# Window attention feeding a mixture of attentions: the weighted values of stage 1 tied to those of stage 2, and the PSUM banks in two rings

## Chip, cores and metric

One Trainium2 chip, one core. Each kernel is one program on that core, inputs and outputs in HBM. The metric is the device time of one execution in microseconds, taken as the median of several executions; a profile is one more execution, recorded by the hardware profiler. The engines are named as in the profile: PE (TensorE, matmuls), PEld (TensorE's weight loads, which overlap PE), DVE (VectorE), ACT (ScalarE), POOL (GpSimd) and SP (SyncE, which issues the transfers). A matmul writes a bank of PSUM; there are eight banks of 128 partitions by 512 fp32 numbers, and only ACT and DVE read them here.

## What is computed

The reference, cut to its core (8 batches, 8 heads, 576 positions, heads of 64, 4 experts of which 2 count for each position):

```
# stage 1: causal attention in a window of 64, on q, k, v
scores = q @ k^T / 8 ; mask: 0 <= row - col < 64
x = softmax(scores) @ v                 # back to batch x 576 x 512
# stage 2: four full causal attentions on x, weighted by a gate
logits = x @ w_gate ; w = softmax over the best 2 of 4
for e in range(4):
    q, k, v = x @ wq[e], x @ wk[e], x @ wv[e]       # 512 -> 64
    a = softmax(q @ k^T / 8, causal over all 576)
    out += w[e] * (a @ v @ wo[e])                   # 64 -> 512
```

## The kernel before

**Stage 1** is cut into 72 groups `g` of four tiles (a tile is 64 query positions of a pair of heads), nine groups to a batch. `s1_qk` multiplies q by k into a PSUM tile `s1` (one bank), adds the mask and finds the row extreme on DVE (L200), takes the exponential on ACT (L210) and scales on POOL (L239). `s1_t` turns two groups' weights with PE transposes into a PSUM tile `t1`, which DVE copies out (L272). `s1_av` multiplies the turned weights by v: a group is eight matmuls (L300), two groups fill one PSUM tile `o1`, and ACT and DVE copy it out as a high and a low part, `xh` (L308) and `xl` (L309).

**Stage 2** takes a batch `b` in two pairs `pr` of experts. `s2_v`, `s2_k` and `s2_q` project `xh` and `xl` (PSUM tiles `v2ps`, `kps`, `qps`; L375 to L377, three matmuls for each product of split operands). `s2_s` makes the scores in eight PSUM tiles `s2` (L502, L503), which DVE masks (L516) and ACT exponentiates. `s2_t` turns the weights with PE transposes (L554, L576) in three tiles `t2` for part 0 of the rows and four for part 1, which ACT copies into `pt` (L561, L567, L578, L583). `s2_av` multiplies these by the values into a tile `o2` (L610), six matmuls for part 0 and ten for part 1, copied out by ACT and DVE as `yh` and `yl` (L616, L617). `s2_o` projects to the output (`ops`).

Both weighted-value steps write 64 rows at a time: their matmuls stand in the profile as `128*64`, all others as `128*128`. Each matmul of L194, L300, L497 and L610 runs as two passes and so has two rows.

**The order.** The last lines of the kernel give each step a time in units of half a batch: stage 2 by the table `POS`, stage 1 by its group number, `LEAD` and `LAG`; the steps are written in that order. A scheduler then orders each engine's instructions and picks the PSUM bank of each tile, out of the ring of its tag. A bank goes to the next tile when the last reader of the tile before is done. `PSB` sets the rings: three banks for `s1` and `s2`, two for `t1` and `t2`, two for the projections (`v2ps`, `kps`, `qps`, `ops`), and one for `o1` and `o2`. The step `s1_av` is moved beside the nearest `s2_av` if that is closer than `NEAR`.

Of the kernel before, what the change touches and what calls it, by code (L numbers as in the profile page):

```python
# [24 lines left out]
POS = {'T00': (-0.009, 0.006), 'T01': (-0.103, 0.133), 'T10': (-0.014, 0.353), 'T11': (0.115, 0.331), 'T1l': (0.403, 0.705), 'A00': (0.082, 0.139), 'A01': (0.077, 0.138), 'A10': (0.417, 0.468), 'A11': (0.358, 0.785), 'A1l': (0.672, 0.695), 'O0': (0.211, 0.52), 'O1': (0.518, 0.918), 'S00': (0.17, 0.403), 'S01': (0.032, 0.316), 'S10': (0.427, 0.819), 'S11': (0.736, 0.891), 'KQ1': (0.0, 1.0), 'V': (0.03, 0.476), 'G': (0.715, 0.852), 'GR': (0.713, 0.723), 'KQ0': (0.439, 0.939), 'VT': (0.084, 0.104)}
PSB = [3, 2, 2, 1]
SNAP = None
MODE = 'fold'
SPREAD = 'APVAVPPP'
LEAD = 12.0  # L30
WPOS = [-0.816, -0.201, -0.2, 1.723]
CPOS = -0.39
NEAR = 0.1
FIRST = 18
# [5 lines left out]
def window_attention_moe_attention(ctx: ExitStack, tc: tile.TileContext, qT, kT, vW,  # L40
# [93 lines left out]

    newer = const.tile([128, 64], mybir.dt.uint32, name="newer")
    nc.vector.tensor_scalar(newer, m_f[:, 0, 64:128], 0.5 * NEG, None, op0=OP.is_gt)

    tri = const.tile([128, 2, 128], F32, name="tri")
# [52 lines left out]
    def s1_qk(g):  # L191
        ps = psum.tile([128, 4, 128], F32, tag="s", bufs=PSB[0], name=f"s1_{g}")
        for i, p, b in tiles(g):
            nc.tensor.matmul(ps[:, i], lhsT=qbd_buf[p % 2][:, b], rhs=pairs[p][1][:, 64 * b:64 * b + 128],  # L194
                             start=True, stop=True)
        st = work.tile([128, 3, 4], F32, tag="st1", bufs=4, name=f"st1_{g}")
        if g < FIRST or MODE == "fold":
            sm = work.tile([128, 4, 2, 64], F32, tag="sm1", bufs=4, name=f"sm1_{g}")
            for i, p, b in tiles(g):
                nc.vector.tensor_tensor_reduce(out=sm[:, i].rearrange("r a c -> r (a c)"), in0=ps[:, i],  # L200
                                               in1=win[:, int(b == 0)], scale=-0.125, scalar=3.0e38,
                                               op0=OP.add, op1=OP.min, accum_out=st[:, 0, i:i + 1])
            if g < FIRST:
                pt = sm.rearrange("r t a c -> r t (a c)")
            else:
                pt = work.tile([128, 4, 64], F32, tag="p1", bufs=4, name=f"p1_{g}")

                nc.vector.tensor_tensor(pt, sm[:, :, 0], sm[:, :, 1], op=OP.min)  # L208
            for i in range(4):
                nc.scalar.activation(pt[:, i], pt[:, i], AF.Exp, bias=st[:, 0, i:i + 1], scale=-1.0,  # L210
                                     accum_out=st[:, 1, i:i + 1])
        else:
            pt = work.tile([128, 4, 64], F32, tag="p1", bufs=4, name=f"p1_{g}")

            firsts = [i for i, p, b in tiles(g) if b == 0]
            cuts = [-1] + firsts + [4]
            for i in firsts:
                nc.gpsimd.memset(pt[:, i], NEG)
            for lo, hi in zip(cuts, cuts[1:]):
                if hi > lo + 1:  # L220
                    nc.scalar.activation(pt[:, lo + 1:hi], ps[:, lo + 1:hi, 0:64], AF.Copy)
            nc.vector.copy_predicated(pt, newer[:, None, :].to_broadcast([128, 4, 64]), ps[:, :, 64:128])
            nc.vector.tensor_reduce(st[:, 0], pt, axis=AX.X, op=OP.max)
            if MODE == "batch":
                nc.gpsimd.tensor_tensor(pt, pt, st[:, 0, :, None].to_broadcast([128, 4, 64]), op=OP.subtract)
                nc.scalar.activation(pt, pt, AF.Exp, scale=0.125)
                nc.vector.tensor_reduce(st[:, 1], pt, axis=AX.X, op=OP.add)
            else:
                nc.vector.tensor_scalar(st[:, 0], st[:, 0], -0.125, None, op0=OP.mult)
                for i in range(4):  # L230
                    nc.scalar.activation(pt[:, i], pt[:, i], AF.Exp, bias=st[:, 0, i:i + 1], scale=0.125,
                                         accum_out=st[:, 1, i:i + 1])
        nc.vector.tensor_scalar_add(st[:, 2], st[:, 1], 1e-9)
        nc.vector.reciprocal(st[:, 2], st[:, 2])  # L234
        if g >= FIRST and MODE == "batch":
            nc.gpsimd.tensor_tensor(pt, pt, st[:, 2, :, None].to_broadcast([128, 4, 64]), op=OP.mult)
        else:
            for i in range(4):
                (nc.vector if g < FIRST and i < 1 else nc.gpsimd).tensor_scalar(pt[:, i], pt[:, i], st[:, 2, i:i + 1],  # L239
                                                                                1.0, op0=OP.mult, op1=OP.mult)  # L240
        P1[g] = pt
        for i, p, b in tiles(g):
            if b == BLK - 1 and p < 2:
                spread_q(p + 2)
            elif b == BLK - 1 and p + 2 < NB * NP:
                load_pair(p + 2)

    def s1_t(g):

        k = g % 9  # L250
        if k % 2 == 0 and k != 8:
            return
        gs = [g - 1, g] if k % 2 else [g]
        t = work.tile([128, 4, 2, 128], F32, tag="pt1", bufs=2, name=f"pt1_{g}")
        if g < FIRST:
            for x, y in enumerate(gs):
                pt = P1.pop(y)
                ps = psum.tile([128, 4, 128], F32, tag="t", bufs=PSB[1], name=f"t1_{y}")
                for i in range(4):
                    nc.tensor.transpose(ps[:, i], pt[:, i], ident)  # L260
                nc.scalar.activation(t[:, 2 * x:2 * x + 2].rearrange("r a e c -> r (a e) c"), ps, AF.Copy)
        else:
            n = 2 * len(gs)
            ps = psum.tile([128, 4, 128], F32, tag="t", bufs=PSB[1], name=f"t1_{g}")
# [223 lines left out]
    def s2_s(b, pr, k):  # L488
# [181 lines left out]
    for g in range(NG1):  # L670
# [76 lines left out]
```

## Time and profile before

| | |
|---|---|
| median of 3 runs | 525.08 us (524.7 to 525.42) |
| the profiled execution | 524.21 us, of which the span from first to last instruction is 522.5 us |
| busy in the span | PE 503.6 us, PEld 447.9, DVE 435.2, ACT 379.7, POOL 229.4 |
| DMA | 51.25 MB, 98 GB/s on average |

How to read it: the busy time of an engine is the time in which it had an instruction in hand. A PE row's end is modelled, and rows overlap in the pipeline, so starts, and steps from one start to the next, say more than durations. Waits are told of the engine that sat idle and of the instruction whose end released it. Where PE waits for an operand or a bank, the wait is longest seen on PEld, whose rows come first.

### The profile page before, as it was taken

To read this page: it belongs to the slowest core of one execution; us is meant where nothing else is said; L and a number is where in the kernel's file an instruction comes from. 1 tells how busy PE (TensorE), PEld (TensorE's weight loads), DVE (VectorE), ACT (ScalarE), POOL (GpSimd) and SP (SyncE) were. 2 spreads that over 40 slices of the span, in tenths; PEclk is the share of its full clock that TensorE was granted. 3 is DMA by queue.
4 is the path that set the end of the run, shared out by engine and by line. 5 is a ranking of instruction groups with operands and counts; after the bars stand their busy time and mean duration, and the time that the engine had idled before them with its cause. 6 is when DMAs were issued, how large, how long until landed. Compare 5 with 4: busy or idle time off the path is not lost.

```text
span 522.5 us, 14102 instructions
## 1 busy us (share of the span) xinstructions
PE 503.6 (96%) x4588; PEld 447.9 (86%) x4588; DVE 435.2 (83%) x1921; ACT 379.7 (73%) x1431; POOL 229.4 (44%) x611
## 2 busy tenths in 40 slices
PE   5999999999999999999999999999999999999996
PEld 5889998888889889988888888988888988998874
DVE  7787888989979898998988988999898998666652
ACT  6998897776676957678495875867767694758572
POOL 8666364444453343622454433444445243233330
PEclk9999999999999999999999999999999999999999
DMA  8963441322613324133341426213261101100103
GB/s 313 299 204 92 146 141 50 92 59 80 180 50 94 115 93 134 44 101 108 112 111 42 127 78 171 88 48 95 87 180 50 46 11 53 41 2 21 62 2 100
DMA packets 49754, 51.25 MB, mean 98 GB/s; under 512 B 35472, under 2 KB 35984, under 8 KB 49680
## 3 DMA queue, kind: packets, MB, share of 16 engines
q1 hardware_dynamic: 49680, 50.35, 32.1%
q8 instruction: 36, 0.59, 0.5%
q14 instruction: 38, 0.31, 0.2%
HBM read 40.90 MB, written 9.44 MB: 96 GB/s over the span
## 4 chain that ended last, share of the span: by engine, by line
PE 61%; ACT 19%; DVE 14%; issue 3%; POOL 1%; DMA 0%; POOLq 0%; DVEq 0%; ACTq 0%
PE o L610 8%; PE s L194 7%; PE t L554 7%; ACT p L210 6%; PE o L300 4%; PE s L502 4%; ACT p L525 3%; PE s L503 3%; PE ops L375 2%; PE kps L376 2%; PE ops L377 2%; PE kps L377 2%; DVE p L516 2%; PE kps L375 2%; PE ops L376 2%
## 5 line engine op out<-in xcount | busy, mean ns | idle before, releaser
L239 POOL TENSOR_SCALAR p<-p,st 128x64 f32<-128x64 f32 x216 | 64.0, 318 | 92.3 <-DVE st L234 54.6
L545 POOL TENSOR_SCALAR p<-p,r 128x192 f32<-128x192 f32 (+3 forms) x128 | 74.6, 597 | 50.0 <-DVE r L541 13.6
L210 ACT ACTIVATE p<-p,st 128x64 f32<-128x64 f32 x216 | 72.3, 337 | 27.1 <-DVE p L208 21.9
L194 PE MATMUL s<-k,qbd 128*128 128x128 f32 x540 | 75.5, 283 | 5.6 <-POOL qbd L94 5.6
L272 DVE TENSOR_TENSOR pt<-t,tri 64x512 f32<-64x512 f32 (+1 forms) x120 | 76.0, 633 | 5.6 <-PE t L268 3.1
L516 DVE CUSTOM_DVE_ANT_0 p<-s,causal 128x320 f32<-128x320 f32 (+3 forms) x160 | 73.4, 471 | 6.3 <-PE s L503 5.0
L200 DVE CUSTOM_DVE_ANT_0 sm<-s,win 128x128 f32<-128x128 f32 x288 | 69.7, 283 | 7.9 <-PE s L194 4.9
L194 PEld LDWEIGHTS s<-k,qbd 128*128 128x128 f32 x540 | 69.8, 197 | 6.6 <-POOL qbd L94 5.6
L554 PE MATMUL t<-ident,p 128*128 128x128 f32 x384 | 59.7, 279 | 3.3 <-ACT pt L567 1.5
L520 ACT ACTIVATE p<-p,r 128x192 f32<-128x192 f32 (+2 forms) x96 | 53.4, 558 | 10.6 <-DVE r L516 10.1
L472 POOL TENSOR_SCALAR qs<-qz 64x256 fp32r<-64x256 f32 x64 | 25.6, 400 | 72.5 <-ACT qz L470 69.0
L610 PE MATMUL o<-pt,v 128*64 128x256 f32 (+3 forms) x512 | 53.5, 340 | 0.9 <-DVE xl L309 0.8
L502 PE MATMUL s<-ks,qz 128*128 128x256 f32 (+2 forms) x160 | 53.4, 345 | 0.4 <-DVE r L516 0.3
L610 PEld LDWEIGHTS o<-pt,v 128*64 128x64 f32 x512 | 36.6, 136 | 19.7 <-ACT pt L578 2.0
L554 PEld LDWEIGHTS t<-ident,p 128*128 128x128 f32 x384 | 42.9, 140 | 11.8 <-ACT pt L583 3.3
L470 ACT ACTIVATE qz<-qps 64x256 fp32r<-64x256 f32 x64 | 24.2, 378 | 34.3 <-DVE qs L471 18.3
L503 PE MATMUL s<-ks,qs 128*128 128x256 f32 (+2 forms) x160 | 48.1, 312 | 0.0
L300 PEld LDWEIGHTS o<-pt,v 128*64 128x64 f32 x1152 | 37.0, 137 | 7.4 <-issue 1.4
L300 PE MATMUL o<-pt,v 128*64 128x64 f32 x1152 | 42.6, 225 | 0.4 <-DVE xl L309 0.3
L210 ACT ACTIVATION_READ_ACCUMULATOR p<-p,st 128x1 f32 x216 | 40.6, 188 | 0.0
L375 PE MATMUL kps<-xh,wkhi 128*128 128x320 f32 (+1 forms) x128 | 39.1, 306 | 0.1
L375 PE MATMUL qps<-xh,wqhi 128*128 128x320 f32 (+1 forms) x128 | 38.6, 302 | 0.2 <-DVE ks L462 0.2
(148 smaller groups left out, 1431.3 us busy)
## 6 DMA issues: line engine op xcount, KB each, us to landing
v<-in_vW_dram SPq DMA_DIRECT2D x32, 576.0 KB, 4.4
k<-in_kT_dram SPq DMA_DIRECT2D x30, 320.0 KB, 3.8
out_dram<-out SPq DMA_DIRECT2D x32, 256.0 KB, 2.2
qbd<-in_qT_dram SPq DMA_DIRECT2D x56, 144.0 KB, 3.5
out_dram<-out SPq DMA_DIRECT2D x8, 128.0 KB, 2.4
p<-in_kT_dram SPq DMA_DIRECT2D x2, 320.0 KB, 7.5
q<-in_qT_dram SPq DMA_DIRECT2D x2, 288.0 KB, 3.5
p<-in_qT_dram SPq DMA_DIRECT2D x2, 288.0 KB, 7.2
```

The lines of the kernel that those rows point to most:

```text
L194: nc.tensor.matmul(ps[:, i], lhsT=qbd_buf[p % 2][:, b], rhs=pairs[p][1][:, 64 * b:64 * b + 128], start=True, stop=True)
L200: nc.vector.tensor_tensor_reduce(out=sm[:, i].rearrange("r a c -> r (a c)"), in0=ps[:, i], in1=win[:, int(b == 0)], scale=-0.125, scalar=3 ...
L210: nc.scalar.activation(pt[:, i], pt[:, i], AF.Exp, bias=st[:, 0, i:i + 1], scale=-1.0, accum_out=st[:, 1, i:i + 1])
L239: (nc.vector if g < FIRST and i < 1 else nc.gpsimd).tensor_scalar(pt[:, i], pt[:, i], st[:, 2, i:i + 1], 1.0, op0=OP.mult, op1=OP.mult)
L272: nc.vector.tensor_mul(t[64 * w:64 * w + 64, :n, e], ps[r, :n], tri[r, w, None, :].to_broadcast([64, n, 128]))
L300: nc.tensor.matmul(o[64 * h:64 * h + 64, 4 * (k % 2) + i], lhsT=pairs[p][2][:, h, b], rhs=t[:, i, 64 * h:64 * h + 64], start=True, stop=True)
L375: nc.tensor.matmul(ps, lhsT=ah, rhs=bh, start=first, stop=False)
L502: nc.tensor.matmul(out, lhsT=QZ[pr][:, e, q], rhs=rhs, start=True, stop=False)
L516: nc.vector.tensor_tensor_reduce(out=dst, in0=ps[:, col:col + n], in1=mask, scale=1.0, scalar=3.0e38, op0=OP.add, op1=OP.min, accum_out=least)
L545: nc.gpsimd.tensor_scalar(p, p, r2[:, 3, x:x + 1], 1.0, op0=OP.mult, op1=OP.mult)
L554: nc.tensor.transpose(ps[:, col:col + 128], P2[part][:, at:at + 128], ident)
L610: nc.tensor.matmul(o[64 * h:64 * h + 64, q0:n], lhsT=V2[b % 2][:, c, 2 * pr + h], rhs=PT2[part][:, h, x:x + w], start=c == 0, stop=c == le ...
```

## The change

Three things, in the planner and in the tags; what is computed is the same.

1. From batch 2 on, four of the five `s1_av` steps of a batch are no longer placed by their own time but directly ahead of an `s2_av` of two batches earlier, in order: 24 pairs. The fifth (`k == 8`) keeps its own time.
2. The four rings become two: five banks for `s1`, `s2` and the projections (tag `s`), three for `t1`, `t2`, `o1` and `o2` (tag `t`).
3. The numbers of the table (`LAG`, `POS`, `LEAD`, `WPOS`, `CPOS`) are others, and branches that were not used (`MODE`, `SNAP`) and the mask `newer`, written by one small DVE instruction at the start, go.

```diff
-LAG = (0.0, 0.07, 0.137)
+LAG = (0.0, 0.112, 0.173)
...
-LEAD = 12.0
-WPOS = [-0.816, -0.201, -0.2, 1.723]
-CPOS = -0.39
-NEAR = 0.1
+LEAD = 12.6
+WPOS = [-0.854, -0.201, -0.2, 1.269]
+CPOS = 0.16
+JOIN8 = 0
...
-        ps = psum.tile([128, 4, 128], F32, tag="s", bufs=PSB[0], name=f"s1_{g}")
+        ps = psum.tile([128, 4, 128], F32, tag="s", bufs=5, name=f"s1_{g}")
...
-            O1[b9] = psum.tile([128, 8, 64], F32, tag="o", bufs=PSB[3], name=f"o1_{g}")
+            O1[b9] = psum.tile([128, 8, 64], F32, tag="t", bufs=3, name=f"o1_{g}")
...
-        ps = psum.tile([128, 512], F32, tag="d", bufs=PSB[2], name=f"{name}ps_{b}_{pr}_{half}")
+        ps = psum.tile([128, 512], F32, tag="s", bufs=5, name=f"{name}ps_{b}_{pr}_{half}")
...
-        if g % 9 % 2 or g % 9 == 8:
-            near = min(bursts, key=lambda x: abs(x - t))
-            if abs(near - t) < NEAR:
-                bursts.remove(near)
-                t = near - 1e-6
+        b, k = g // 9, g % 9
+        if b >= 2 and (k % 2 == 1 or k == 8 and JOIN8):
+            t = bursts[4 * (b - 2) + min(k // 2, 3)] - 1e-6 + (k == 8) * 1e-7
```

Each engine runs the same instructions as before (but for `newer`), in another order. Three places of PE's order show it. In the names, `o2_1_0_1` is the tile of batch 1, pair 0, part 1, and a last number counts the buffers; lines of the kernel after are some 30 smaller, so L610 is L579, L300 is L269, L554 is L523, L375 is L344.

First, the weighted values of batch 1, pair 0, part 1. Before, four score matmuls and four of a projection stand between the burst of stage 1 and that of stage 2:

```order
L300 MATMUL o1_27_2527<-pt1_28_2353,v12_1992 64x64 x16
L194 MATMUL s1_32_2563<-k14_2243,qbd0_67 128x128 x4
L375 MATMUL kps_2_0_0_2586<-xh2_1548,wkhi_605 128x320
L376 MATMUL kps_2_0_0_2586<-xl2_1549,wkhi_605 128x320
L377 MATMUL kps_2_0_0_2586<-xh2_1548,wklo_606 128x320
L375 MATMUL kps_2_0_0_2586<-xh2_1548,wkhi_605 128x320
L610 MATMUL o2_1_0_1_2548<-pt2_1_136,v2_1_150 64x256 x6
L610 MATMUL o2_1_0_1_2548<-pt2_1_136,v2_1_150 64x192 x2
L610 MATMUL o2_1_0_1_2548<-pt2_1_136,v2_1_150 64x64 x2
L376 MATMUL kps_2_0_0_2586<-xl2_1549,wkhi_605 128x320
```

After, the two are one burst, behind the last transposes:

```order
L523 MATMUL t2_1_0_1_3_2639<-ident_90,p2_1_70 128x128 x4
L269 MATMUL o1_29_2647<-pt1_30_2511,v12_1958 64x64 x2
L269 MATMUL o1_29_2647<-pt1_30_2511,v13_2187 64x64 x14
L579 MATMUL o2_1_0_1_2668<-pt2_1_134,v2_1_148 64x256 x6
L579 MATMUL o2_1_0_1_2668<-pt2_1_134,v2_1_148 64x192 x2
L579 MATMUL o2_1_0_1_2668<-pt2_1_134,v2_1_148 64x64 x2
L344 MATMUL kps_2_0_1_2683<-xh2_1486,wkhi_573 128x256
```

The program has 73 such bursts of 64-row matmuls before, with none of `o1` and `o2` together, and 49 after, of which 24 hold both.

Second, the transposes of batch 2, pair 0, part 1. Before, `t2_2_0_1_1` and the next tile, `t2_2_0_1_2`, have the same bank, and ten matmuls of a projection stand between them (the first and the last are shown):

```order
L268 MATMUL t1_39_3557<-ident_90,p1_39_3274 128x128 x2
L554 MATMUL t2_2_0_1_1_3566<-ident_90,p2_1_70 128x128 x4
L375 MATMUL qps_3_0_0_3578<-xh3_2528,wqhi_609 128x320
...
L375 MATMUL qps_3_0_0_3578<-xh3_2528,wqhi_609 128x320
L554 MATMUL t2_2_0_1_2_3572<-ident_90,p2_1_70 128x128 x4
L376 MATMUL qps_3_0_0_3578<-xl3_2529,wqhi_609 128x320
```

After, they have two banks, and the bank of `t2_2_0_1_2` was last that of `t2_2_0_1_0`, two tiles back:

```order
L188 MATMUL s1_42_3545<-k19_3376,qbd1_68 128x128
L523 MATMUL t2_2_0_1_1_3572<-ident_90,p2_1_70 128x128 x4
L344 MATMUL v2ps_3_3_3578<-wvhi_440,xh3_2421 128x260
...
L346 MATMUL v2ps_3_3_3578<-wvhi_440,xl3_2422 128x260
L523 MATMUL t2_2_0_1_2_3597<-ident_90,p2_1_70 128x128 x4
L344 MATMUL qps_3_0_0_3603<-xh3_2421,wqhi_577 128x320
```

Twelve matmuls of a projection now stand between the two, and the second no longer needs the first one's bank.

Third, the output projection behind the weighted values of batch 1, pair 1, part 1. Before, it follows directly:

```order
L610 MATMUL o2_1_1_1_3078<-pt2_1_136,v2_1_150 64x64 x2
L375 MATMUL ops_1_2_3093<-wohi_1254,yh0_141 128x512
L376 MATMUL ops_1_2_3093<-wolo_1255,yh0_141 128x512
L377 MATMUL ops_1_2_3093<-wohi_1254,yl0_143 128x512
L375 MATMUL ops_1_2_3093<-wohi_1254,yh1_142 128x512
```

After, scores, a burst of stage 1 and a projection come first:

```order
L579 MATMUL o2_1_1_1_3126<-pt2_1_134,v2_1_148 64x64 x2
L188 MATMUL s1_38_3141<-k16_2591,qbd0_67 128x128
L188 MATMUL s1_38_3141<-k17_2870,qbd1_68 128x128 x3
...
L346 MATMUL qps_2_1_1_3197<-xh2_1486,wqlo_578 128x256
L188 MATMUL s1_39_3216<-k17_2870,qbd1_68 128x128 x4
L344 MATMUL ops_1_2_3239<-wohi_1127,yh0_139 128x512
```

So the copies `yh` and `yl` now have those matmuls' time.

More of the change, by code (lines that the diff above doesn't have):

```diff
@@ L23 @@
 MERGE = 1
-LAG = (0.0, 0.07, 0.137)
[L25 to L28, printed above, removed]
+LAG = (0.0, 0.112, 0.173)
+POS = {'T00': (-0.037, 0.001), 'T01': (-0.184, 0.013), 'T10': (0.259, 0.759), 'T11': (0.441, 0.455), 'T1l': (0.455, 0.705), 'A00': (0.095, 0.13), 'A01': (0.069, 0.16), 'A10': (0.424, 1.024), 'A11': (0.358, 0.924), 'A1l': (0.695, 0.733), 'O0': (0.228, 0.52), 'O1': (0.926, 1.002), 'S00': (0.093, 0.454), 'S01': (-0.073, 0.268), 'S10': (0.427, 0.812), 'S11': (0.736, 0.997), 'KQ1': (-0.217, 0.972), 'V': (0.01, 0.683), 'G': (0.875, 0.924), 'GR': (0.805, 1.047), 'KQ0': (0.43, 0.93), 'VT': (-0.022, 0.005)}
 SPREAD = 'APVAVPPP'
-LEAD = 12.0
-WPOS = [-0.816, -0.201, -0.2, 1.723]
-CPOS = -0.39
-NEAR = 0.1
+LEAD = 12.6
+WPOS = [-0.854, -0.201, -0.2, 1.269]
+CPOS = 0.16
+JOIN8 = 0
 FIRST = 18
@@ L133, in window_attention_moe_attention @@
     make_identity(nc, ident)
-    newer = const.tile([128, 64], mybir.dt.uint32, name="newer")
-    nc.vector.tensor_scalar(newer, m_f[:, 0, 64:128], 0.5 * NEG, None, op0=OP.is_gt)
     tri = const.tile([128, 2, 128], F32, name="tri")
@@ L196, in s1_qk @@
         st = work.tile([128, 3, 4], F32, tag="st1", bufs=4, name=f"st1_{g}")
[L197 to L211, printed above, removed]
+        sm = work.tile([128, 4, 2, 64], F32, tag="sm1", bufs=4, name=f"sm1_{g}")
@@ L212, in s1_qk @@
+        for i, p, b in tiles(g):
+            nc.vector.tensor_tensor_reduce(out=sm[:, i].rearrange("r a c -> r (a c)"), in0=ps[:, i],
+                                           in1=win[:, int(b == 0)], scale=-0.125, scalar=3.0e38,
+                                           op0=OP.add, op1=OP.min, accum_out=st[:, 0, i:i + 1])
+        if g < FIRST:
+            pt = sm.rearrange("r t a c -> r t (a c)")
         else:
             pt = work.tile([128, 4, 64], F32, tag="p1", bufs=4, name=f"p1_{g}")
-            firsts = [i for i, p, b in tiles(g) if b == 0]
@@ L216, in s1_qk @@
[L216 to L232, printed above, removed]
+            nc.vector.tensor_tensor(pt, sm[:, :, 0], sm[:, :, 1], op=OP.min)
@@ L233, in s1_qk @@
+        for i in range(4):
+            nc.scalar.activation(pt[:, i], pt[:, i], AF.Exp, bias=st[:, 0, i:i + 1], scale=-1.0,
+                                 accum_out=st[:, 1, i:i + 1])
         nc.vector.tensor_scalar_add(st[:, 2], st[:, 1], 1e-9)
         nc.vector.reciprocal(st[:, 2], st[:, 2])
[L235 to L239, printed above, removed]
+        for i in range(4):
+            (nc.vector if g < FIRST and i < 1 else nc.gpsimd).tensor_scalar(pt[:, i], pt[:, i], st[:, 2, i:i + 1],
@@ L257, in s1_t @@
                 pt = P1.pop(y)
-                ps = psum.tile([128, 4, 128], F32, tag="t", bufs=PSB[1], name=f"t1_{y}")
+                ps = psum.tile([128, 4, 128], F32, tag="t", bufs=3, name=f"t1_{y}")
                 for i in range(4):
@@ L263, in s1_t @@
             n = 2 * len(gs)
-            ps = psum.tile([128, 4, 128], F32, tag="t", bufs=PSB[1], name=f"t1_{g}")
+            ps = psum.tile([128, 4, 128], F32, tag="t", bufs=3, name=f"t1_{g}")
             for x, y in enumerate(gs):
@@ L379, in s2_v @@
     def s2_v(b, j):
-        ps = psum.tile([128, 512], F32, tag="d", bufs=PSB[2], name=f"v2ps_{b}_{j}")
+        ps = psum.tile([128, 512], F32, tag="s", bufs=5, name=f"v2ps_{b}_{j}")
         for c in range(NP):
@@ L492, in s2_s @@
         r2, m2 = R2[b, pr], M2[b, pr]
-        ps = psum.tile([128, 512], F32, tag="s", bufs=PSB[0], name=f"s2_{b}_{pr}_{k}")
+        ps = psum.tile([128, 512], F32, tag="s", bufs=5, name=f"s2_{b}_{pr}_{k}")
         for i, e, col, key, n in BANKS[k]:
@@ L547, in s2_t @@
     def s2_t(b, pr, part, k):
-        ps = psum.tile([128, 512], F32, tag="t", bufs=PSB[1], name=f"t2_{b}_{pr}_{part}_{k}")
+        ps = psum.tile([128, 512], F32, tag="t", bufs=3, name=f"t2_{b}_{pr}_{part}_{k}")
         pt = PT2[part]
@@ L606, in s2_av @@
         n = 64 * (b1 - b0)
-        o = psum.tile([128, 512], F32, tag="o", bufs=PSB[3], name=f"o2_{b}_{pr}_{part}")
+        o = psum.tile([128, 512], F32, tag="t", bufs=3, name=f"o2_{b}_{pr}_{part}")
         for c, (x, w, q0) in enumerate(AVS[part]):
@@ L619, in s2_o @@
     def s2_o(b, j):
-        ps = psum.tile([128, DM], F32, tag="d", bufs=PSB[2], name=f"ops_{b}_{j}")
+        ps = psum.tile([128, DM], F32, tag="s", bufs=5, name=f"ops_{b}_{j}")
         for pr in range(2):
@@ L688, in window_attention_moe_attention @@
             load_v(2)
-    if SNAP:
-        todo = SNAP(todo, s2_av)
     for _, f, args in sorted(todo, key=lambda x: x[0]):
```

## The prediction

> **What bounds it now.** I read the page first, then one stretch of the steady state by windows, then PE's timeline at a few places, and last the waits of PEld.
>
> ```profile
> span 522.5 us, 14102 instructions
> ...
> PE 503.6 (96%) x4588; PEld 447.9 (86%) x4588; DVE 435.2 (83%) x1921; ACT 379.7 (73%) x1431; POOL 229.4 (44%) x611
> ```
>
> PE is the bound: 503.6 of 522.5 us busy, so every microsecond off PE's stream is nearly one off the time. But busy is not the same as streaming, and what lies inside those 96% is the question. The engine that comes next is DVE, and in the steady state it is closer than the page's average says. Columns: stretch, its length, then busy time of PE, PEld, DVE, ACT and POOL.
>
> ```profile
> 210.00:270.00 60.00, 58.69 (x549) 52.38 (x548) 54.52 (x229) 42.79 (x168) 26.82 (x68) 1.00 0.32 95
> ```
>
> DVE has 60 - 54.52 = 5.5 us left in these 60, and the granted clock is 1.00, so the clock plays no part.
>
> **Switches between 64-row and 128-row matmuls.** PE's timeline (start, duration, instruction) around two bursts of `o1`, one of 32 passes and one of 16, and a burst of `o2`:
>
> ```profile
> 150.36 1.15 PE L300 MATMUL o<-pt,v 128*64 128x64 f32 x32
> 151.44 1.16 PE L194 MATMUL s<-k,qbd 128*128 128x128 f32 x8
> ...
> 152.87 0.30 PE L375 MATMUL kps<-xh,wkhi 128*128 128x320 f32 x1
> 153.57 1.96 PE L610 MATMUL o<-pt,v 128*64 128x256 f32 x20 [0.40 <-DVE xl L309]
> 155.46 0.41 PE L376 MATMUL kps<-xl,wkhi 128*128 128x320 f32 x1
> 155.71 0.31 PE L377 MATMUL kps<-xh,wklo 128*128 128x320 f32 x1
> 155.85 0.31 PE L375 MATMUL kps<-xh,wkhi 128*128 128x320 f32 x1
> ```
>
> ```profile
> 260.63 0.28 PE L376 MATMUL qps<-xl,wqhi 128*128 128x256 f32 x1
> 260.75 0.28 PE L377 MATMUL qps<-xh,wqlo 128*128 128x256 f32 x1
> 260.96 0.69 PE L300 MATMUL o<-pt,v 128*64 128x64 f32 x16
> 261.58 1.09 PE L554 MATMUL t<-ident,p 128*128 128x128 f32 x8
> ```
>
> From first start to the next group's start, 32 passes take 151.44 - 150.36 = 1.08 us and 16 take 261.58 - 260.96 = 0.62. Sixteen passes are thus worth 0.46, and 0.16 of each burst is fixed. On the way in, the last step before the burst is 0.21 (260.75 to 260.96) where its like is 0.12: 0.09 more. On the way out, the first 128-row step of a projection is 0.25 (155.46 to 155.71) where the next is 0.14: 0.11 more, though not each follower need pay that. A burst so costs 0.16 + 0.09 = 0.25 us without and 0.36 with the last part, all of it inside "busy". I take 0.30.
>
> By the program's order, 73 bursts become 49. 24 x 0.30 = 7.2 us less (24 x 0.25 = 6.0 to 24 x 0.36 = 8.6). Unknown is what the step from `o1` to `o2` inside a joined burst costs, since none exists before. Its nearest rows: nothing, as within the burst at 150.36, or the 0.09 of the way in, 24 x 0.09 = 2.2 us. I take nothing, because the height of 64 rows doesn't change there, and keep 6.0 - 2.2 = 3.8 as the lower end.
>
> The Trainium skill, TensorEngine Tiling (Array Packing), Key Properties, says that changing the tiling mode, not just the tile, drains TensorE; it gives no price. The trace's 0.25 to 0.36 us for each burst agrees, and by that rule the step inside a joined burst is free, as I took it.
>
> **Waits for a bank.** A place that shows one, all engines of interest in order of time:
>
> ```profile
> 216.97 0.60 PE L554 MATMUL t<-ident,p 128*128 128x128 f32 x4
> ...
> 218.73 0.31 PE L375 MATMUL qps<-xh,wqhi 128*128 128x320 f32 x1
> 218.99 0.58 ACT L583 ACTIVATE pt<-t 128x512 f32<-128x512 f32 x1
> ...
> 219.63 0.42 PEld L554 LDWEIGHTS t<-ident,p 128*128 128x128 f32 x4 [0.85 <-ACT pt L583]
> 219.63 0.66 PE L554 MATMUL t<-ident,p 128*128 128x128 f32 x4 [0.59 <-ACT pt L583]
> ```
>
> The transposes at 219.63 don't need what ACT copies; they need its bank. ACT copies at 218.99 to 219.57 the tile written at 216.97, and 0.06 us later PE goes on: a step of 0.90 (218.73 to 219.63) where 0.14 is normal. PEld's list names such waits by who ended them: total, times, longest.
>
> ```profile
> PEld t L554 <- ACT pt L583: 3.3, 7, 0.9
> PEld t L554 <- ACT pt L567: 3.0, 6, 0.8
> PEld t L576 <- ACT pt L567: 2.1, 6, 0.4
> PEld o L610 <- ACT pt L578: 2.0, 7, 0.4
> PEld o L610 <- DVE xl L309: 1.7, 3, 0.7
> PEld ops L377 <- DVE yl L617: 1.7, 7, 0.3
> ...
> PEld s L502 <- DVE r L516: 1.3, 5, 0.5
> PEld v2ps L376 <- DVE wvlo L176: 1.2, 1, 1.2
> ...
> PEld o L610 <- ACT pt L561: 1.0, 3, 0.4
> ```
>
> Banks are the transposes behind ACT's `pt` (3.3 + 3.0 + 2.1), `o2` behind DVE's `xl` (1.7: the single bank of tag `o`; this is the 0.40 at 153.57) and scores behind DVE's reading of scores (1.3): 11.4 us.
>
> Does the new order part them? I walked PE's order with the bank of each tile, and added up these steps (0.12 to 0.14 for a projection's matmul, some 0.11 for a transpose, 0.06 for two passes of `o1`) from the end of a tile's last matmul to the first of the next tile in its bank. This is an estimate of distance, not of time waited. Under 1.5 us after a `t2` tile: 23 of 110 before, 2 of 110 after. Under 2.5 us after an `s2` tile: 13 before, 2 after. ACT needed from 217.57 (end of the tile's rows) to 219.57, so 2.0 us, at the place shown; after, 18 of 110 `t2` distances are under 2.0 (33 before). I take two thirds of the 11.4 back: 7.6 us. The ends are nothing (every wait only changes its releaser) and 11.4.
>
> What holds `o1` can hurt instead: its two readers follow each other.
>
> ```profile
> 151.56 0.60 ACT L308 ACTIVATE xh<-o 128x512 fp32r<-128x512 f32 x1 [0.25 <-PE o L300]
> 152.84 0.68 DVE L309 TENSOR_TENSOR xl<-o,xh 128x512 fp32r<-128x512 f32 x1
> ```
>
> The burst's next start was 151.44, the bank is free at 153.52, so 2.1 us. In the new order the next tile in a joined `o1`'s bank comes 4.1 us later at the least. No charge.
>
> **Waits for operands.** `ops` behind `yl` (1.7) is the third place of the order shown: the distance from the last `o2` matmul to `ops` (the same sum of steps) was under 1.3 us at fifteen of the 36 tiles and is so at one, and over 4 us at 28; all 1.7 go. `o2` behind a copy of its own `pt` (2.0 + 1.0) is softened, since in a joined burst the `o1` passes, 0.92 us for 32 at 0.46 for 16, stand between the last transposes and `o2`. Half, 1.5, goes. Such a wait also sits inside a burst, where the list doesn't see all of it:
>
> ```profile
> 347.05 2.44 PE L610 MATMUL o<-pt,v 128*64 128x256 f32 x20
> 349.42 0.47 PE L502 MATMUL s<-ks,qz 128*128 128x448 f32 x1
> ```
>
> Twenty passes take 349.42 - 347.05 = 2.37 us here, and 155.46 - 153.57 = 1.89 above. I add nothing for it; it is a margin on the good side. Sum: 3.2 us, ends 0 and 4.7.
>
> **The start.** The first `v2ps` matmul waits 1.2 us for the low half of its weights (L176). It stands some 5 us of matmuls later in the new order, since `LEAD` is larger and stage 2 begins behind more of stage 1. I take 1.0 of 1.2, with 0 and 1.2 as ends. The constants of stage 2 (`CPOS`) stand at the same places of POOL's queue at the start, and `newer` is one small DVE instruction beside PE's work: nothing. SP issues as many transfers as before, and the loads follow the same stage-1 groups: nothing.
>
> **What is late next.** With 7.2 + 7.6 + 3.2 + 1.0 = 19.0 us less, DVE's spare time in 60 us would fall from 5.5 by 60 x 19.0 / 522.5 = 2.2 to 3.3. What waits remain of the rows above, 17.3 - 11.8 = 5.5 us, I let grow as the spare time shrinks, by 5.5 / 3.3 = 1.67: 3.7 us more, again between 0 and the whole of the 11.8.
>
> Sum: 19.0 - 3.7 = 15.3 us. From the profiled execution's 524.21 that is 508.9; it is 0.9 under the median of 525.08, and against the median I say 525.1 - 15.3 = 509.8, rounded to 510.
>
> **Rivals.**
> - Only the switches pay. Banks are freed by DVE and ACT, and if these are late, more banks and longer distances only move the wait to the next operand; the 91% of DVE in the window above speaks for it, the 5.5 us that it has left against it. Then 525.1 - 7.2 = 517.9. The same page of the Trainium skill, PSUM Bottleneck, says that tiling speeds up TensorE but not the copies out of PSUM. The window's DVE figure agrees that these are the next bound, and by that rule the result is this rival.
> - The join saves nothing: the step from `o1` to `o2` costs a whole switch, say because the `o2` half waits inside the burst with `o1` already done. Then 525.1 - (15.3 - 7.2) = 517.0. For it speaks the burst of 2.37 us above; against it that this burst waits as long without a join.
> - All of it goes: 8.6 + 11.4 + 4.7 + 1.2 = 25.9, 499.2. Against it is DVE.
> - Slower: three banks for transposes and values. A joined burst takes two of the three, and transposes next to it must do with one until `yh` and `yl` are out. It decides from 15.3 / 24 = 0.64 us for each joined burst; at 1.0 us, as the longest bank waits of the list (0.9) would have it, the time is 525.1 - 15.3 + 24.0 = 533.8. For it: `o1` keeps a bank 2.1 us beyond its matmuls. Against it: the distances of 4.1 us.
>
> **Chances.** The sum as told 0.50, all of it 0.08, only the switches 0.24, no gain from the join 0.06, slower by the three banks 0.08, and 0.04 that gains and new waits cancel. A change of 0.2%, 1.05 us, is about what a measurement of this kernel can tell from none. So faster 0.88, same 0.04, slower 0.08. I predict 510 us. The range goes from all of it, rounded up to 500, to the rival of the switches alone with 2 us for its uncertain price, 520; it leaves out the slower cases, the cancelled ones and half of the best.
>
> **What would show it.** In the profile after, 24 bursts of `o` should read as L269 followed at once by L579, with no more than 0.1 us more than their parts' passes. PEld's waits for ACT's `pt` should fall from 8.4 us to about 3, `o` behind `xl` to about 0, `ops` behind `yl` to under 0.5. DVE should have some 93 to 95% in the steady state. I am wrong if PEld's list shows the same total with other names, or transposes waiting for `yl` or `xl`, which would be the three banks.

## The result, and the profile after

The kernel after takes 503.91 us (median of 4 runs, 503.82 to 504.26), the kernel before 524.99 beside it (524.70 to 525.42): a ratio of 0.9599, interval 0.9582 to 0.9616, so 21.1 us less, where 15.3 were forecast. The profiled execution took 503.99 us. By the starts of the same `o2` bursts in both traces, the gain is spread over the run: 3 us at 202, 9 at 322, 13 at 380, 17 at 446 and 20 at 491.

The profile's page, span and busy time of the engines:

```profile
span 502.3 us, 14147 instructions
...
PE 485.2 (97%) x4588; PEld 443.9 (88%) x4588; DVE 434.3 (86%) x1920; ACT 378.7 (75%) x1431; POOL 233.3 (46%) x611
```

PE's busy time is 18.4 us less with the same 4588 matmuls, and its share rose to 97%. So most of what was saved had been called busy. DVE and ACT do what they did, in a shorter span.

The steady state by windows (stretch, length, busy PE, PEld, DVE, ACT, POOL):

```profile
210.00:270.00 60.00, 59.56 (x574) 54.76 (x574) 56.29 (x235) 46.04 (x181) 28.14 (x74) 1.00 0.33 100
```

In the same 60 us PE gets through 574 rows where it was 549, and DVE has 56.29 us of work, 94%.

PEld's waits (total, times, longest; the rows of 0.2 us or more add up to 24.2 us here and to 36.7 before):

```profile
PEld s L188 <- POOL qbd L91: 5.7, 1, 5.7
PEld t L523 <- ACT pt L552: 4.5, 6, 0.9
PEld o L269 <- issue: 2.5, 14, 0.2
...
PEld t L523 <- DVE xl L278: 0.8, 1, 0.8
...
PEld o L579 <- ACT pt L547: 0.5, 2, 0.4
PEld o L579 <- ACT pt L552: 0.3, 2, 0.2
...
PEld o L579 <- ACT pt L557: 0.3, 1, 0.3
PEld ops L344 <- ACT yh L585: 0.2, 1, 0.2
```

The first row is the program's start and was there before (5.6). Of the waits that the prediction listed, one kind is left with a size: transposes behind ACT's `pt`, 4.5 us. `ops` behind `yl` (1.7), scores behind DVE's `r` (1.3) and the first `v2ps` (1.2) have no row any more.

A joined burst on PE's timeline:

```profile
95.42 1.15 PE L269 MATMUL o<-pt,v 128*64 128x64 f32 x32
96.40 1.91 PE L579 MATMUL o<-pt,v 128*64 128x256 f32 x20
98.24 0.38 PE L344 MATMUL kps<-xh,wkhi 128*128 128x256 f32 x1
98.46 0.28 PE L345 MATMUL kps<-xl,wkhi 128*128 128x256 f32 x1
98.58 0.28 PE L346 MATMUL kps<-xh,wklo 128*128 128x256 f32 x1
```

From first start to the follower's start it takes 98.24 - 95.42 = 2.82 us; apart, the two took 1.08 and 1.89, so 2.97. The step inside the burst costs nothing, and the fixed 0.15 is paid once. On the way out the first step of the projection is 0.22 (98.24 to 98.46) where the next is 0.12.

### The profile page after: what moved, and what is told of

Same layout as the page of the kernel before. It is cut to its first block, busy times and chain, and to the rows that moved or that the text cites. A ratio compares the mean times of both kernels' runs of the same rounds, so it can differ in the third digit from the quotient of the medians.

```text
span 502.3 us, 14147 instructions
## 1 busy us (share of the span) xinstructions
PE 485.2 (97%) x4588; PEld 443.9 (88%) x4588; DVE 434.3 (86%) x1920; ACT 378.7 (75%) x1431; POOL 233.3 (46%) x611
## 4 chain that ended last, share of the span: by engine, by line
PE 73%; DVE 13%; ACT 9%; issue 2%; DMA 1%; POOL 0%; SPq 0%; ACTq 0%; DVEq 0%; POOLq 0%
PE o L579 8%; PE s L188 8%; PE t L523 7%; PE o L269 6%; PE s L471 5%; PE s L472 4%; PE kps L344 3%; PE kps L346 3%; ACT p L203 3%; PE kps L345 3%; DVE pt L241 3%; PE qps L344 3%; PE v2ps L346 3%; PE v2ps L344 3%; PE v2ps L345 3%; PE qps L345 3%
## 5 line engine op out<-in xcount | busy, mean ns | idle before, releaser
L208 POOL TENSOR_SCALAR p<-p,st 128x64 f32<-128x64 f32 x216 | 66.1, 328 | 50.1 <-DVE st L206 22.4
L188 PE MATMUL s<-k,qbd 128*128 128x128 f32 x540 | 73.1, 280 | 6.1 <-POOL qbd L91 5.8
L241 DVE TENSOR_TENSOR pt<-t,tri 64x512 f32<-64x512 f32 (+1 forms) x120 | 76.0, 634 | 2.4
L485 DVE CUSTOM_DVE_ANT_0 p<-s,causal 128x320 f32<-128x320 f32 (+3 forms) x160 | 72.2, 472 | 6.4 <-PE s L472 4.0
L193 DVE CUSTOM_DVE_ANT_0 sm<-s,win 128x128 f32<-128x128 f32 x288 | 71.4, 283 | 6.6 <-PE s L188 4.1
L188 PEld LDWEIGHTS s<-k,qbd 128*128 128x128 f32 x540 | 67.6, 195 | 7.0 <-POOL qbd L91 5.7
L523 PE MATMUL t<-ident,p 128*128 128x128 f32 x384 | 55.5, 275 | 2.6 <-ACT pt L552 2.0
L471 PE MATMUL s<-ks,qz 128*128 128x256 f32 (+2 forms) x160 | 54.8, 352 | 0.3 <-DVE ks L431 0.3
L523 PEld LDWEIGHTS t<-ident,p 128*128 128x128 f32 x384 | 44.6, 141 | 8.5 <-ACT pt L552 4.5
L579 PE MATMUL o<-pt,v 128*64 128x256 f32 (+3 forms) x512 | 50.3, 335 | 0.2 <-ACT pt L557 0.2
L579 PEld LDWEIGHTS o<-pt,v 128*64 128x64 f32 x512 | 35.6, 137 | 13.1 <-ACT pt L547 0.5
L269 PE MATMUL o<-pt,v 128*64 128x64 f32 x1152 | 43.4, 226 | 0.6 <-ACT pt L230 0.4
L269 PEld LDWEIGHTS o<-pt,v 128*64 128x64 f32 x1152 | 37.2, 137 | 7.2 <-issue 2.5
L430 ACT ACTIVATE ks<-kps 64x320 fp32r<-64x320 f32 (+1 forms) x64 | 25.9, 404 | 21.4 <-DVE ks L431 17.3
L344 PE MATMUL qps<-xh,wqhi 128*128 128x320 f32 (+1 forms) x128 | 39.5, 308 | 0.0
L344 PE MATMUL kps<-xh,wkhi 128*128 128x320 f32 (+1 forms) x128 | 39.3, 307 | 0.0
```

What stands on the lines that cost most here:

```text
L269: nc.tensor.matmul(o[64 * h:64 * h + 64, 4 * (k % 2) + i], lhsT=pairs[p][2][:, h, b], rhs=t[:, i, 64 * h:64 * h + 64], start=True, stop=True)
L344: nc.tensor.matmul(ps, lhsT=ah, rhs=bh, start=first, stop=False)
L471: nc.tensor.matmul(out, lhsT=QZ[pr][:, e, q], rhs=rhs, start=True, stop=False)
L485: nc.vector.tensor_tensor_reduce(out=dst, in0=ps[:, col:col + n], in1=mask, scale=1.0, scalar=3.0e38, op0=OP.add, op1=OP.min, accum_out=least)
L523: nc.tensor.transpose(ps[:, col:col + 128], P2[part][:, at:at + 128], ident)
L579: nc.tensor.matmul(o[64 * h:64 * h + 64, q0:n], lhsT=V2[b % 2][:, c, 2 * pr + h], rhs=PT2[part][:, h, x:x + w], start=c == 0, stop=c == le ...
```

## The experiments

The theory at the start was that of the prediction: fewer switches, more distance for banks and operands, each paying by itself. The rivals were that one of the parts does nothing, and that "switch" is a name for something else. In what follows, bursts are the runs of 64-row matmuls in PE's order (73 before, 49 after, 24 of them joined), and "the list" is the sum of PEld's waits as above. The times stand against 524.6 to 524.9 us for the kernel before beside them.

**The rings undone** (positions and the rule that joins stay):

```diff
-tag="s", bufs=5   # s1, s2
+tag="s", bufs=3
-tag="s", bufs=5   # v2ps, kps, qps, ops
+tag="d", bufs=2
-tag="t", bufs=3   # t1, t2
+tag="t", bufs=2
-tag="t", bufs=3   # o1, o2
+tag="o", bufs=1
```

> The kernel after with the four rings of before (3, 2, 2, 1); positions and join rule stay. By the program's order no burst of stage 1 and stage 2 is joined any more (74 bursts of 64-row matmuls instead of 49), and 15 re-uses of a bank behind a t2 tile lie under 1.5 us of matmuls, against 2. Theory A (joins are worth 0.30 us each and need a second bank for o; banks cost by short distances): 503.9 + 25 x 0.30 + some 5 us of bank waits = 516 (512 to 520). Rival B (the rings alone are the gain, order does not matter): 525. Rival C (the positions alone are the gain): 504 to 506.

Measured: 524.09 us (523.58 to 524.73), ratio 0.9983 [0.9973, 0.9992]; the list is 39.8. With a single bank for `o1` and `o2` the scheduler joins none: 74 bursts, 0 joined. Its waits:

```profile
PEld o L579 <- DVE xl L278: 5.1, 13, 0.7
PEld o L269 <- issue: 4.0, 21, 0.3
PEld t L523 <- ACT pt L552: 3.5, 13, 0.4
```

`o2` now stands close behind `o1` in the same bank and waits for `xl` 13 times (3 times before the change). So without the rings the new positions, with a rule that puts `o1` ahead of an `o2` in the same bank, are worth 0.8 us, not 9. The positions without that rule were not run on the old rings.

**The rings alone** (the kernel before, with tags and counts of the kernel after):

> The kernel before with the rings of five and three, and nothing else. The order has 71 bursts (3 joined), 14 re-uses of a bank behind a t2 tile under 1.5 us (23 before). Theory A: 525.0 - 0.6 for two bursts less - 3 to 5 us of the bank waits = 520 (517 to 523). Rival B (rings alone are the gain): 504 to 508. Rival C (positions alone): 525.

Measured: 525.02 us (524.27 to 527.16), ratio 1.0009 [0.9997, 1.0022]: no change. 71 bursts, 3 joined; the list is 38.8:

```profile
PEld o L610 <- ACT pt L578: 5.3, 10, 0.9
PEld t L576 <- ACT pt L567: 3.8, 6, 0.8
PEld s L502 <- ACT qf L476: 2.7, 3, 0.9
```

Against the prediction's list of before, the wait of `o2` for `xl` is gone, `ops` behind `yl` fell from 1.7 to 1.1, and `o2` behind its own `pt` rose from 2.0 to 5.3. Here the waits did little but change their releaser.

**The rings and the join with the old positions** (the kernel before, rings of five and three, the rule that joins, and `LEAD` 12.6, since the join needs stage 1 further ahead):

> The kernel before with the two rings and the join rule, and its old positions except LEAD = 12.6 (the join rule needs stage 1 that far ahead). The order has 53 bursts (24 joined), but 26 re-uses of a bank behind a t2 tile under 1.5 us, more than before the change (23). Theory A: 503.9 + 4 x 0.30 + 8 us of bank waits + 2 us of operand waits = 515 (511 to 519). Rival: joins and rings are all, positions do not matter: 505. Rival B' (short distances do not cost with three banks): 506 to 508.

Measured: 528.24 us (527.92 to 528.45), ratio 1.0062 [1.0047, 1.0077]: slower than before, with 53 bursts and 24 joined. The list is 43.6:

```profile
PEld t L576 <- ACT pt L567: 5.3, 12, 0.7
PEld t L554 <- POOL p L545: 4.0, 15, 0.4
PEld o L610 <- ACT pt L561: 3.1, 4, 1.1
```

Twenty bursts fewer (some 6 us) are lost again, and the list is 6.9 longer than before: transposes wait for banks behind ACT's copies (`pt`, 12 times) and for their own weights (`p`, 15 times).

**The rule that joins taken out** of the kernel after:

```diff
-        if b >= 2 and (k % 2 == 1 or k == 8 and JOIN8):
-            t = bursts[4 * (b - 2) + min(k // 2, 3)] - 1e-6 + (k == 8) * 1e-7
```

> The kernel after without the join rule; rings of five and three and positions stay. The order has 61 bursts (6 joined by chance) and the same distances between re-uses of a bank. Theory A: 12 bursts more at 0.30 us = 3.6, so 507.5 (506 to 509). Rival: the join mainly covers the copy that o2 waits for (an o1 burst between the transposes and o2), then up to 0.5 us more at each of the 18 unjoined, 512 to 517. Rival B (rings alone): 504.

Measured: 508.43 us (508.26 to 508.67), ratio 0.9686 [0.9671, 0.9700]. In the trace twelve of the 61 bursts hold both tiles, half of the 24: six with `o1` ahead, which the expectation counts, and six with `o2` ahead. So rings and positions, with half of the joins, give 16.5 us, and the rule adds 4.5: twelve bursts at 0.28 (3.4) and 1.3 us of the list (25.5 against 24.2). The transposes behind ACT's `pt` L552 have no row here; a wait of much the same size stands at scores some 11 us ahead of them, at as many places:

```profile
PEld s L471 <- PE t L545: 5.3, 6, 0.9
```

**What a switch costs.** A small matmul on 128 rows, ahead of each `o2`, parts the joined bursts; the same as two halves of 64 rows doesn't. Both write columns of the bank that are not read.

```diff
+        nc.tensor.matmul(o[:, 448:512], lhsT=ident, rhs=ident[:, 0:64], start=True, stop=True)
```

```diff
+        for h in range(2):
+            nc.tensor.matmul(o[64 * h:64 * h + 64, 448:512], lhsT=ident[:, 0:64], rhs=ident[:, 0:64], start=True, stop=True)
```

> The kernel after with one small 128-row matmul (identity by 64 columns of it, into columns of the o2 bank that nothing reads) ahead of each of the 32 o2 tiles. In the 24 joined bursts it stands between o1 and o2 and parts them: 73 bursts instead of 49, everything else in place. Theory A (a change between 64-row and 128-row matmuls costs 0.30 us for each burst): 503.9 + 32 x 0.11 for the matmuls + 24 x 0.30 = 514.6 (512 to 517), that is 7 us above the next kernel. Rival (the saving of a join lies in the waits that it covers, and a switch is cheap): 507 to 509, as the next kernel.

> The control to the kernel before: the same small matmul as two 64-row halves, so that the joined bursts stay joined (50 bursts). Both theories: 503.9 + 32 x 0.12 for four passes of 0.03 = 507.7 (505 to 509). What counts is the difference to the kernel before: 7 us by theory A, under 1 by the rival.

Measured: 513.08 us (512.33 to 514.58) with the switch, ratio 0.9780 [0.9758, 0.9802], 73 bursts; 506.90 (506.17 to 508.62) without, ratio 0.9663 [0.9642, 0.9685], 50 bursts. The 23 bursts cost 6.2 us, 0.27 each. PE's timeline at the same burst, with the switch and then without:

```profile
96.06 1.15 PE L269 MATMUL o<-pt,v 128*64 128x64 f32 x32
97.15 0.43 PE L577 MATMUL o<-ident 128*128 128x64 f32 x2
97.51 1.96 PE L580 MATMUL o<-pt,v 128*64 128x256 f32 x20
99.40 0.38 PE L344 MATMUL kps<-xh,wkhi 128*128 128x256 f32 x1
```

```profile
95.23 1.15 PE L269 MATMUL o<-pt,v 128*64 128x64 f32 x32
96.21 0.29 PE L578 MATMUL o<-ident 128*64 128x64 f32 x4
96.33 1.91 PE L581 MATMUL o<-pt,v 128*64 128x256 f32 x20
98.17 0.39 PE L344 MATMUL kps<-xh,wkhi 128*128 128x256 f32 x1
```

From `o1` to the projection it is 99.40 - 96.06 = 3.34 us against 98.17 - 95.23 = 2.94, so 0.40 at the place; some of that comes back, since the list is 4.1 shorter with the switches (17.5 against 21.6): a PE that is later waits less. So 0.27 in the time and 0.40 on PE's stream, with the prediction's 0.30 between. The rival, that a switch is only how waiting looks (under 1 us for all), is out. The rule quoted in the prediction from the Trainium skill, TensorEngine Tiling (Array Packing), Key Properties, that a change of mode drains TensorE, fits this cost, and so does its other half, not just the tile: 64-row matmuls of two tiles follow each other at no charge. What happens inside TensorE at a switch no trace shows.

**More work for DVE**, to try the term "What is late next": one memset per group of stage 1.

```diff
+        extra = work.tile([128, 256], F32, tag="extra", bufs=2, name=f"extra_{g}")
+        nc.vector.memset(extra, 0.0)
```

> The kernel after with one more DVE instruction in each of the 72 groups of stage 1, a memset of 128x256 that nothing reads (0.27 us for that form at the start of the kernel before: 19.4 us more on DVE, 11.6 of it between 90 and 390 us, where DVE has 17.5 us to spare). Theory A (PE's stream bounds the kernel and DVE's spare time, though small, absorbs it): 504 to 508. Rival (DVE bounds as well, what it gets more comes out in the time): 516 to 524. The prediction's own rule (remaining waits, 18 us, grow as DVE's spare time shrinks, here from 3.5 to 1.2 us in 60): 539.

Measured: 511.49 us (510.88 to 511.66), ratio 0.9744 [0.9730, 0.9759], so 7.6 more than the kernel after. The memsets' row (duration least, median and most in ns, first and last start), and one wait:

```profile
L206 DVE MEMSET extra<- x72: 272/272/272, 4.4 to 161.1; 128x256 f32 x72
```

```profile
PEld t L231 <- DVE sm L210: 4.5, 1, 4.5
```

The memsets use no data, so the scheduler put them early: 57 of the 72 run before 90 us, the last at 161. That is another load than meant, most of it on the start, and the wait of 4.5 us (0.8 in the kernel after) belongs to it. Behind this wait the granted clock is 0.50 from 16 to 19 us, and behind one of 2.0 us again from 37 to 39, where the kernel after has 1.00. By PE's timeline the bursts of `o2` are 5.8 us later than in the kernel after at 82 us and 5.9 at 96, but 7.6 at 109 and 7.6 at the end. In between stand ten of the other fifteen memsets, within 7.5 us, and a projection waits for DVE:

```profile
109.09 0.43 DVE L433 TENSOR_TENSOR ks<-kps,ks 64x256 fp32r<-64x256 f32 x1
109.66 0.36 PE L346 MATMUL qps<-xh,wqhi 128*128 128x256 f32 x1 [1.38 <-DVE ks L433]
```

PEld waits 1.6 us here; in the kernel after this projection has no wait, and DVE is busy 7.67 of the 8.40 us that this stretch takes there (95.4 to 103.8). So 2.7 us of memsets, where DVE had 0.7 to spare, cost 1.6 us or so. By the prediction's rule, waits that grow as DVE's spare time shrinks, the time would have been 539. The rule says far too much here, but the theory that DVE costs nothing (504 to 508) missed too, and what an even load costs stays open.

**Positions of the waiting transposes.** The 4.5 us left are six waits at one place of the order, in six of the batches; here is one on the timeline of PE and ACT:

```profile
295.43 0.33 ACT L203 ACTIVATE p<-p,st 128x64 f32<-128x64 f32 x1
...
296.43 0.33 ACT L203 ACTIVATE p<-p,st 128x64 f32<-128x64 f32 x1
...
296.88 0.38 ACT L439 ACTIVATE qz<-qps 64x256 fp32r<-64x256 f32 x1
...
297.28 0.35 ACT L489 ACTIVATE px<-px,r 128x64 f32<-128x64 f32 x1
...
297.55 0.39 PE L346 MATMUL ops<-wohi,yl 128*128 128x512 f32 x1
297.75 1.09 ACT L552 ACTIVATE pt<-t 128x512 f32<-128x512 f32 x2
...
298.40 1.14 PE L523 MATMUL t<-ident,p 128*128 128x128 f32 x8 [0.46 <-ACT pt L552]
```

If the short distance on PE is the cause, spreading these transposes ends the wait:

```diff
-'T11': (0.441, 0.455)
+'T11': (0.39, 0.47)
```

> The kernel after with the four part-1 transposes of pair 1 spread: T11 from (0.441, 0.455) to (0.39, 0.47). The largest wait that is left in the kernel after is transposes for a bank that ACT still copies (4.5 us, 6 times), at two pairs of transposes that stand 1.83 us of matmuls apart; in the new order 8 distances behind a t2 tile are under 2 us instead of 18, with the same 49 bursts. Theory A (short distances in a ring are the waits): five of the six go, 3.7 us, 500.2 (499 to 502). Rival (the wait moves to the next operand or bank, as it did with the rings alone): 503 to 505.

Measured: 506.77 us (505.64 to 507.76), ratio 0.9659 [0.9636, 0.9683], so 2.9 slower than the kernel after, with 49 bursts and 24 joined as there. Distances under 2.0 us fell from 18 to 8, by the count that the prediction uses, and the wait nearly doubled:

```profile
PEld t L523 <- ACT pt L552: 8.6, 6, 1.6
```

```profile
297.79 0.38 ACT L439 ACTIVATE qz<-qps 64x256 fp32r<-64x256 f32 x1
298.19 0.35 ACT L489 ACTIVATE px<-px,r 128x64 f32<-128x64 f32 x1
...
298.65 1.09 ACT L552 ACTIVATE pt<-t 128x512 f32<-128x512 f32 x2
```

At this place the whole kernel runs 0.9 us later than the kernel after, and ACT's copy with it (298.65 against 297.75): it still stands behind the same `qz` and `px`. The waiting transposes are now written behind three matmuls of `ops` instead of six, so they ask for the bank 0.7 us earlier against the copy, and the longest wait is 0.7 longer (1.6 against 0.9), though the distance from the bank's last tile is no shorter (about 2.0 us, at the line of the count, against 1.83). A bank comes free when its reader's turn in ACT's queue has come; a distance on PE that is counted without that turn does not tell the wait. A distance far beyond the turn was not tried in a kernel with the same data flow.

**The copies moved to DVE**, all with `k < 2` of pair 1 and part 1, and then those with `k == 0` alone:

```diff
+            if pr == 1:             # second kernel: if pr == 1 and k == 0:
+                nc.vector.tensor_copy(pt[:, k, 0:512], ps)
+            else:
                 nc.scalar.activation(pt[:, k, 0:512], ps, AF.Copy)
```

> The kernel after with the first two part-1 transposes of pair 1 copied out by DVE instead of ACT (16 copies of 128x512). Each of the six waits left for a bank (4.5 us in all) falls where ACT has four exponentials, a copy of qz and one more exponential ahead of these copies. Theory A' (a bank is free when its reader has had its turn in its engine's queue): the waits behind ACT's copy go, 503.9 - 4.5 + 1 to 3 for 11 us more on DVE = 501 to 503. Rival (DVE has no turn to give either, and its own queue makes the transposes wait as long or longer): 505 to 510. Joined bursts stay at 24 of 49.

> As the kernel before it, but only the first of the two copies goes to DVE, so that ACT and DVE copy the two tiles side by side (8 copies). Theory A': half to all of the 4.5 us go, with half the load on DVE: 500.5 to 503. Rival (DVE has no turn to give): 504 to 507.

Measured: 511.60 us (510.93 to 512.43), ratio 0.9756 [0.9739, 0.9773], and 506.10 (505.95 to 507.83), ratio 0.9653 [0.9635, 0.9671]. Both are slower than the kernel after. With the first, a wait behind ACT's `qf` is new:

```profile
PEld kps L344 <- ACT qf L445: 5.0, 5, 1.0
```

With the second, two rows stand where there was one, and the moved copy comes late:

```profile
PEld t L523 <- ACT pt L555: 4.5, 6, 0.9
PEld t L523 <- DVE pt L241: 4.2, 5, 0.8
```

```profile
302.07 0.65 DVE L553 COPY pt<-t 128x512 f32<-128x512 f32 x1
```

DVE's queue has no turn free at this place either: its 0.7 us pieces of L241 stand ahead of the copy, which starts 6.0 us after the transposes of its tile (296.08). The scheduler gave the waiting transposes other banks: the first pair waits for ACT's copy of the other tile as before, the second for L241, which reads a `t1` tile out of the bank that it gets.

**Rings of four and four** in the kernel after:

```diff
-tag="s", bufs=5
+tag="s", bufs=4
-tag="t", bufs=3
+tag="t", bufs=4
```

> The kernel after with two rings of four banks instead of five and three; positions and joins stay. A fourth bank for the transposes and values leaves 2 of 110 distances behind a t2 tile under 2 us (18 before this edit), but the order then has 59 bursts (24 joined) and 14 distances behind an s2 tile under 2.5 us (2). Theory A': a wait for a bank lasts until its reader's turn in its engine's queue, so a bank more removes the 4.5 us of transposes behind ACT's copy: 503.9 - 4.5 + 10 x 0.28 for ten bursts more + 1 to 3 for the scores = 504.5 (502 to 507). Rival (positions fit one pair of rings, and any other ring brings new waits as large as with the old rings): 512 to 524.

Measured: 515.25 us (514.70 to 515.59), ratio 0.9824 [0.9809, 0.9839]; 59 bursts, 24 joined; the list is 28.8:

```profile
PEld o L269 <- DVE pt L241: 4.7, 7, 0.7
...
PEld s L471 <- DVE out L595: 3.0, 3, 1.0
```

The transposes no longer wait behind L552, as a fourth bank should make it, but the scheduler's order is another, with ten bursts more (some 3 us) and new waits. With this other pair of rings the same table of positions is 11 us slower.

**Late transposes.** The last two transposes of pair 1, part 1, are written 0.10 later. They then come behind the first two masked scores of the next step, which go into the same buffer that they read, so part of what they turn is the next step's weights: the time is of the same instructions, not of the same data flow.

```diff
+                wait = 0.10 if late == "1" and k > 1 else 0.0
+                it.append((n + lo + (hi - lo) * (k + 0.5) / 4 + wait, s2_t, (zb, zp, 1, k)))
```

> The kernel after with the last two of the four part-1 transposes of pair 1 written 0.10 later. They then come long after ACT's copies of the first two (3.7 and 8.2 us of matmuls instead of 1.8), and six bursts fewer stand in the order (43, 24 joined), but distances under 1.5 us behind a t2 tile go from 2 to 8 and behind an s2 tile under 2.5 us from 2 to 9. Theory A': the six waits of 0.75 us go (4.5), six bursts are saved (1.7), and new short distances give back 2 to 5: 501 (498.5 to 504). Rival (any move off the tuned positions loses more than it gains): 506 to 515.

Measured: 535.73 us (535.19 to 536.82), ratio 1.0222 [1.0204, 1.0241], with only 43 bursts, the fewest of all, and a list of 50.6:

```profile
PEld s L471 <- issue: 14.4, 5, 2.9
PEld kps L344 <- ACT qf L445: 6.3, 5, 1.3
```

```profile
320.67 0.36 PE L471 MATMUL s<-ks,qz 128*128 128x256 f32 x1 [2.64 <-DVE ks L431]
```

Scores lose 14.4 us at five places, once in a batch, for which the list names no releaser; PE's own rows name DVE's `ks`, and their bank was last that of a `kps` tile, which `ks` reads. Why DVE comes so late there, and how much of it the changed data flow adds, was not tried. After each of the five waits the granted clock (the 0.50 in this row) is halved for some 3 us, and once more near 452 us:

```profile
322.00:324.00 2.00, 2.00 (x12) 2.00 (x11) 0.75 (x6) 1.37 (x8) 0.73 (x2) 0.50 0.01 4
```

By the mean clock, 0.981 of 533.5 us, that is some 9 of the 32 us that this kernel is slower than the kernel after (0.998 of 502.3 there). So neither theory of the expectation is tested by it.

## Why the prediction was right, and where it was off

The time, 503.9, lies in the range of 500 to 520, and for the change as a whole the mechanism of the likeliest case (switches and waits both pay) is the one seen. Term by term, from the list of before and of after; only the switches have an experiment of their own, the other rows are an account from the list:

| term | forecast | found |
|---|---|---|
| switches | -7.2 | 24 x 0.27 to 0.30: -6.5 to -7.2 |
| waits for a bank | -7.6 of 11.4 | 11.4 to 4.5 + 0.8: -6.1 |
| waits for operands | -3.2 of 4.7 | 4.7 to 0.5 + 0.3 + 0.3 + 0.2: -3.4 |
| the start | -1.0 of 1.2 | 1.2 to 0: -1.2 |
| what is late next | +3.7 | the rest of the list, 36.7 - 17.3 = 19.4, to 24.2 - 6.6 = 17.6: -1.8 |
| not in the list | 0 | -1.4 to -2.1, what is left of 21.1 |

The sum is 15.3 forecast and 21.1 found.

- **What is late next** is the term that was mis-sized: 3.7 us to be given back, where nothing was. DVE's load rose as said (93 to 95% forecast, 94% found), but nothing waited more for it. A rule drawn from one number, waits growing as spare time shrinks, had no row behind it. That DVE is no bound at all isn't shown either: where ten memsets fell into a stretch in which DVE had 0.7 us to spare, PE waited 1.6 us. The rule of the Trainium skill, TensorEngine Tiling (Array Packing), PSUM Bottleneck, that copies don't get faster with TensorE, would have made it 517.9; the copies did not get faster, and the time is 14 us below that, because there was room for them.
- **Switches.** Right in size; the step inside a joined burst is free, so the lower end of 3.8 and the rival "the join saves nothing" fall. The kernel without the rule takes 508.43, 4.5 us more, though, not 7.2: half of the joins, 73 bursts to 61, come with rings and positions.
- **Waits for a bank.** The total was near, the piece behind ACT's `pt` wasn't: 8.4 to 4.5, where about 3 were said. The prediction read a bank's return from the distance along PE's order. The spread transposes show what it left out: the place of the reader in its own engine's queue (0.7 us earlier against ACT's copy, 0.7 us more wait).
- **Waits for operands and the start** went as said, and the 0.8 left behind `xl` is one transpose, not the values.
- **The slower rival**, three banks, didn't show: in the kernel after no transpose waits for `yl`, and one for `xl`. A kernel with all the joins and these rings can be slower than before all the same (528.24): with the old positions its transposes wait 5.3 us for banks behind ACT's copies and 4.0 for their own weights. How much of that is the three banks isn't shown.
- **What the prediction had as a sum holds only for the whole.** It added up terms as if rings, positions and join each paid. Rings alone take 525.0, positions and the rule on the old rings (where nothing joins) 524.1, rings and the rule on the old positions 528.2, rings and positions with half of the joins 508.4, all three 503.9. The reading of the list told what was there to be won; that rings and positions are both needed for it no single row told. That the sum came near is luck in that respect: its terms hold for the whole change and not as prices of its parts.

A rough rule, bursts x 0.28 plus the list, gives the differences to the kernel after within 2.5 us for before, the rings undone, the rings alone and the rule taken out. It is some 4 us short for rings and join with the old positions and for four and four, and also for the switch itself (2.3 of 6.2 us, as the 0.27 already holds the shorter list). Waits inside PE's bursts, which the list doesn't see, are a likely reason; that was not tried. Left open is which numbers of the table make the new order good: the positions were tried as a whole, and at two places, both of which made it slower. No kernel tried was faster than the one with the change.

## What to carry to other kernels

A PE that is 96% busy can still lose time inside the busy share: compare one step from start to start with its undisturbed like, and count changes of tile shape in PE's order. Rings of banks, the order of the work and the place of each reader in its engine's queue are one design; changing one alone mostly passes a wait on to another name, so predict a bundle from the order that it gives, not by adding up its parts. A term for "the next engine becomes late" needs a row that shows waits rising with its load, as the ten memsets give for one stretch; a share of 94% is none.

## What was not expected of the hardware

- DVE ran at 94% in the steady state (56.29 of 60 us) and no kind of wait behind it had more than 0.8 us in the list.
- A PE that is held up by switches waits less elsewhere: with 23 more bursts the list fell from 21.6 to 17.5 us, so that 0.40 us on PE's stream is 0.27 us in the time.
- The granted clock fell to 0.50 for some 3 us behind each of the five waits of 2.88 us of the kernel with the late transposes (322 to 325 us behind the one that ends at 320.64) and behind the wait of 4.48 us with the memsets (16 to 19 us). Behind the waits of up to 1.8 us in the kernel after and in the spread one it stayed at 1.00, and behind the first wait of 5.7 us too; behind one of about 2 us it fell with the memsets and not in the kernel with two 64-row halves. By mean it was 0.981 and 0.991 in the two profiles with such falls, 0.997 to 1.000 in the others. That the waits bring it down was not tried by itself.
